# A causal convolution of two runs moved from TensorE to VectorE and GpSimd in a fused attention and gated-linear kernel

## The chip, the cores and the metric

One core of one Trainium2 chip. The metric is device time in microseconds of one execution. Engines are named as the profile names them: PE is TensorE, DVE is VectorE, ACT is ScalarE, POOL is GpSimd, SP is SyncE, which here issues nearly all transfers.

## The reference

Blockwise causal attention over 8 batches, 8 heads, 576 positions and 64 elements per head, then a gated linear unit whose gate comes from a causal depthwise convolution of 5 taps.

```
scores = (q @ k^T) / 8, masked to key block <= query block (blocks of 64)
attn   = softmax(scores) @ v
x      = attn with heads joined: [8, 576, 512]
gate   = sigmoid( sum over k of conv_w[k] * x shifted by 4-k )      # 5 taps per channel
out    = (gate * (x @ w_val)) @ w_out                                # [8, 576, 512], fp32
```

Inputs and output are fp32. The kernel works in fp16 with fp32 accumulation.

## The kernel before, in words

The whole kernel is written out as one list, `PLAN` (lines 12 to 109). Each word of it is one step, name/arguments/engine/banks, and the list is walked once (line 668), so each engine runs its steps in the order in which the list has them. PSUM banks are written into the list too; a step that needs a bank waits until the step that reads the bank's last content is done.

Work on attention goes by pairs of heads, 32 of them: pair p is batch p // 4 and heads 2(p % 4) and the next.

- `lk`, `lq` (line 244), `lv` (260), `lt` (267, the last 64 positions of all heads of a batch, two transfers for q and two for k), `lvt` (274): loads, all issued by SyncE but one (`lq/1`, by ScalarE at the start). The staging tiles rotate: five buffers for q and k, five for v.
- `cq`, `cv`, `ct`, `cvt` (line 232): casts to fp16, mostly on GpSimd.
- `T`, `TT` (141): transposes of q and k on TensorE; `Te`, `TTe` copy them out of PSUM (VectorE or ScalarE).
- `S` (three parts a pair) and `SL`: scores; `E`, `EL` (442, 457): exponentials on ScalarE; `mka`, `mkb` (464 to 470): masking memsets on GpSimd.
- `A`, `AT`: weighted sums with a column of ones that gives the denominator; `N`, `NT` (491, 492): normalization on VectorE; `X`, `XT` and `Xe`, `XTe`: transposes into `xt`.

`xt` holds channels in partitions and positions in a ring of four batches, each with four columns of zeros ahead of it. Work on the gated unit goes by runs of 464 columns of this ring; there are ten runs, n = 0 to 9. Partition 32x + i of group g in `xt` is channel 128g + 32x + i, and the columns of the value and output matrices are ordered to suit the convolution's output (line 383 and the function `W`), where tile x holds the channels of row group x from all four g.

- `C` (line 585): the convolution of a run on TensorE: for each tap 16 matmuls of 32 x 32 blocks with diagonal weights `DG`, 80 in all, into four banks.
- `CS` (598): tanh on ScalarE of two banks at a time into `th` (three buffers, fp32); the sigmoid is made from it.
- `V` (604): value projection, one bank for each of four parts x; `Ve` (612): (th + 1) * value on VectorE into `gv`, which frees the bank.
- `O`, `OL`: output projection from `gv`; `Oe`, `OLe`: copy out of PSUM; `Od`, `OLd`: stores, on SyncE's queue among the loads.
- `w0`: a matmul of zeros that keeps TensorE going; six in the list.

In what follows a step is written as in the list without engine, as in `V/9.3` or `T/30`. Taps of the convolution read `xt` from column 464 (n % 5) on.

Of the kernel before, what the change touches and what calls it, by code (L numbers as in the profile page):

```python
# [17 lines left out]
w0/1.64.1/P/5 E/1.0/A cq/4/V cq/3/V lvt/0/S E/0.2/A lv/2.0/S T/4/P/0+1 lq/8/S lk/8/S lq/7/S
S/1.1/P/2+3 E/1.1/A lk/7/S T/3/P/4+5 S/1.2/P/6+7 E/1.2/A Te/4/V S/4.0/P/0+1 lv/4.1/S T/2/P/2+3
E/4.0/A Te/3/V S/3.1/P/4+5 E/3.1/A mkb/0/G S/3.0/P/6+7 cv/0/G A/0/P/0+1 E/3.0/A S/4.1/P/4+5 Te/2/V  # L20
S/3.2/P/2+3 N/0/V mka/1/G cv/1/V ct/1/G cq/5/G TT/1/P/6+7 TTe/1/V w0/1.64.0/P/0 S/2.2/P/0+1 ct/2/G
E/4.1/A mkb/1/G mka/4/G E/3.2/A X/0/P/4+5 cv/3/G Xe/0/V E/2.2/A cq/6/G mkb/3/G mkb/2/G cvt/0/G
cv/2/G lv/7.0/S lv/5.0/S lv/4.0/S lwv/1/S S/2.1/P/2+3 E/2.1/A lwv/0/S lwo/0/S lwo/1/S T/5/P/4+5
Te/5/V lk/9/S lq/9/S lv/6.0/S lv/5.1/S cq/8/G lv/6.1/S lq/10/S lk/10/S mka/3/G cq/7/G lk/12/S
lq/12/S S/4.2/P/6+7 E/4.2/A mkb/4/G w0/1.64.0/P/0 S/2.0/P/0+1 E/2.0/A SL/1/P/2+3 EL/1/A A/1/P/4+5
N/1/V TT/2/P/6+7 TTe/2/V S/5.0/P/0+1 S/5.2/P/2+3 T/6/P/4+5 Te/6/V lq/13/S X/1/P/6+7 Xe/1/V E/5.0/A
lv/7.1/S lvt/1/S E/5.2/A mkb/5/G AT/0/P/0 NT/0/V lk/11/S lk/13/S lq/11/S S/6.1/P/4+5 S/6.0/P/6+7
SL/2/P/2+3 E/6.0/A EL/2/A T/8/P/0+1 Te/8/V A/3/P/6+7 N/3/V S/5.1/P/2+3 E/6.1/A T/7/P/0+1 Te/7/V
S/8.2/P/4+5 mka/2/G A/2/P/6+7 S/7.1/P/0+1 N/2/V E/5.1/A cwv/1/G cwv/0/G mka/5/G mka/6/G cwo/0/G
X/3/P/2+3 Xe/3/V E/8.2/A X/2/P/6+7 S/6.2/P/4+5 Xe/2/V E/7.1/A S/8.0/P/2+3 E/6.2/A cq/9/G mkb/8/G  # L30
E/8.0/A cv/5/G mkb/6/G cv/4/V C/0/P/0+1+6+7 A/4/P/4+5 XT/0/P/2 V/0.0/P/3 CS/0.1/A N/4/V X/4/P/4+5
CS/0.0/A Xe/4/A Ve/0.0/V S/7.0/P/0+1 E/7.0/A cwo/1/V XTe/0/V V/0.3/P/7 mka/7/G Ve/0.3/V V/0.2/P/3
Ve/0.2/V cv/6/G W//P/0+1+4+5 We/1/V S/7.2/P/6+7 V/0.1/P/2 We/0/A T/9/P/0+1 Te/9/V E/7.2/A
S/8.1/P/4+5 E/8.1/A A/5/P/6+7 S/9.0/P/0+1 A/6/P/4+5 Ve/0.1/V O/0.1/P/2 N/5/V E/9.0/A N/6/V X/5/P/0+1
Xe/5/A cq/10/G T/10/P/6+7 Te/10/V cq/12/G S/9.1/P/4+5 E/9.1/A O/0.2/P/3 Oe/0.2/V T/12/P/0+1 Te/12/V
S/10.0/P/6+7 mkb/7/G cv/7/G E/10.0/A cvt/1/G S/10.1/P/4+5 E/10.1/A O/0.0/P/3 X/6/P/6+7 Xe/6/A
Oe/0.0/A mka/8/G Oe/0.1/A lt/3.0/S lt/3.1/S A/7/P/0+1 AT/1/P/4 lv/8.0/S lt/4.0/S lt/4.1/S
S/12.0/P/6+7 mka/9/G lv/8.1/S N/7/V X/7/P/0+1 NT/1/V cq/11/G Xe/7/V lv/10.1/S E/12.0/A XT/1/P/5
XTe/1/V lv/10.0/S S/9.2/P/2+3 T/11/P/0+1 Te/11/V C/1/P/4+5+6+7 E/9.2/A cq/13/G T/13/P/2+3 V/1.1/P/0
CS/1.0/A lv/9.1/S Te/13/V lv/9.0/S lvt/2/S lv/11.1/S CS/1.1/A S/11.0/P/4+5 S/11.2/P/2+3 ct/3/G  # L40
TT/3/P/6+7 mkb/9/G TTe/3/V Ve/1.1/V cv/8/G V/1.3/P/1 Ve/1.3/V E/11.0/A lv/11.0/S lk/15/S
S/13.2/P/6+7 lq/15/S E/11.2/A S/10.2/P/4+5 mka/10/G lk/16/S V/1.0/P/0 Ve/1.0/V E/13.2/A A/8/P/2+3
N/8/V S/11.1/P/6+7 ct/4/G TT/4/P/0+1 TTe/4/V cv/10/G lq/16/S E/10.2/A lk/14/S lq/14/S V/1.2/P/5
Ve/1.2/V mkb/10/G mkb/11/G A/10/P/2+3 N/10/V mkb/13/G SL/3/P/0+1 E/11.1/A S/13.0/P/6+7 EL/3/A cv/9/G
E/13.0/A cvt/2/G A/9/P/4+5 X/8/P/0+1 Xe/8/A cv/11/G AT/2/P/2 S/12.1/P/6+7 E/12.1/A X/10/P/0+1 N/9/V
mka/11/G A/11/P/4+5 Xe/10/A O/0.3/P/3 NT/2/V XT/2/P/2 XTe/2/A lq/17/S SL/4/P/0+1 EL/4/A cq/15/G
T/15/P/6+7 N/11/V lk/17/S lv/13.1/S Oe/0.3/V S/13.1/P/4+5 Te/15/V O/0.4/P/2 S/12.2/P/0+1 lv/13.0/S
# [6 lines left out]
S/14.1/P/2+3 E/14.1/A Te/18/V V/2.0/P/0 Ve/2.0/V lk/19/S lk/20/S lq/20/S Od/0.2/S lv/16.1/S cv/13/G
mka/13/G A/13/P/4+5 N/13/V S/17.1/P/6+7 Oe/0.5/A mkb/15/G cvt/3/G E/17.1/A S/17.2/P/2+3 V/2.1/P/0
Ve/2.1/V cv/14/G mkb/14/G mka/14/G A/14/P/4+5 S/17.0/P/6+7 cv/12/G E/17.2/A E/17.0/A lv/16.0/S
S/16.2/P/0+1 E/16.2/A N/14/V lq/21/S mkb/12/G A/12/P/2+3 cv/15/G N/12/V lk/21/S ct/5/G AT/3/P/5
S/18.1/P/6+7 E/18.1/A S/16.1/P/2+3 TT/5/P/0+1 TTe/5/V cq/19/G Od/0.1/S lv/18.1/S lt/6.1/S cq/20/G
E/16.1/A mka/16/G cv/16/G O/1.0/P/4 Oe/1.0/V mkb/16/G A/15/P/6+7 T/19/P/0+1 Te/19/A Od/0.4/S
# [24 lines left out]
S/26.1/P/6+7 E/26.1/A NT/5/V V/5.0/P/2 A/23/P/0+1 SL/6/P/6+7 EL/6/A Te/29/V cq/28/G S/26.2/P/3+4
# [28 lines left out]
def kernel(  # L113
# [44 lines left out]
    def one(b):  # L158
        return PS[0:128, b]
# [562 lines left out]
```

## Time and profile before

| | before |
|---|---|
| times of the runs | 186.05, 187.36, 188.68 us (median 187.36) |
| profiled execution: time / span | 188.06 / 186.3 us |
| busy PE / DVE / ACT / POOL | 164.2 / 125.1 / 137.0 / 82.7 us |
| mean granted TensorE clock | 0.972 |
| moved by DMA | 40.38 MB, mean 217 GB/s |
| C: 800 matmuls of 32 x 464 | 13.1 us busy |
| tanh of a half run (`CS`) | 20, mean 945 ns |

The span runs from the first to the last instruction; the time is longer than the span by what the runtime does around it. In the profile's groups, "x40 | 24.6, 633 | 13.1" reads: 40 instructions, 24.6 us busy, 633 ns each, 13.1 us of idle time on the engine just before them, followed by what ended that idle time. A timeline line gives the start and the duration in us, engine, line, operation, tile written <- tiles read. SPq is SyncE's queue: the instruction there issues a transfer, it does not last until the transfer has landed.

### The profile page before, as it was taken

The page shows a single profiled execution, that of the slowest core. Times are in us where ns is not written, and L with a number is a line of the kernel's source. Part 1 is how long each engine was busy: PE and PEld are TensorE (multiplying, and loading weights), DVE is VectorE, ACT ScalarE, POOL GpSimd, SP SyncE. Part 2 cuts the span into 40 slices and gives each one's busy share as a digit, 9 for nine tenths or more (in the row PEclk, how much of TensorE's full clock was granted, in tenths as well). Part 3 has the DMA queues.
Part 4 walks back from the last instruction along what each step waited for, and adds up shares of the span by engine and source line. Part 5 has one row for each costly group of instructions (what it writes and reads, how often), then busy time and mean ns, then how long its engine had stood idle before and what let it go on. Part 6 is the DMA issues. An engine that isn't in the chain of part 4 may idle for free.

```text
span 186.3 us, 8262 instructions
## 1 busy us (share of the span) xinstructions
PE 164.2 (88%) x3534; PEld 101.4 (54%) x3534; DVE 125.1 (67%) x223; ACT 137.0 (74%) x164; POOL 82.7 (44%) x198
## 2 busy tenths in 40 slices
PE   1587638889999996999999999999999999999991
PEld 0364417754565774467645564656665575565540
DVE  5676636749977886777854677799787587533731
ACT  4489963698699885999969998897999842453431
POOL 6206449265682754556407455757590360000000
PEclk9999975699999999999999999999999999999999
DMA  6897896998966899769968888999998110351175
GB/s 184 261 286 180 223 262 172 291 328 243 267 165 157 224 308 300 191 165 327 273 157 272 239 245 260 298 286 282 222 276 231 69 60 0 141 204 57 69 281 217
DMA packets 66493, 40.38 MB, mean 217 GB/s; under 512 B 40213, under 2 KB 60949, under 8 KB 66458
## 3 DMA queue, kind: packets, MB, share of 16 engines
q1 hardware_dynamic: 66186, 39.61, 74.2%
q8 instruction: 27, 0.44, 1.0%
q10 hardware_dynamic: 272, 0.26, 0.4%
q14 instruction: 8, 0.07, 0.1%
HBM read 30.42 MB, written 9.44 MB: 214 GB/s over the span
## 4 chain that ended last, share of the span: by engine, by line
PE 74%; DMA 8%; DVE 5%; ACT 4%; SPq 4%; issue 3%; POOL 1%; DVEq 0%; ACTq 0%; POOLq 0%
PE PS L137 66%; PE PS L141 8%; DMA qks<-in_q_dram 3%; DMA qks<-in_k_dram 3%; ACT pt L442 3%; DMA vs<-in_v_dram 2%; DVE qkT L232 2%; SPq L244 2%; SPq L267 1%; DVE x L492 1%; ACT qkT L230 1%; POOL qk L232 1%; DVE rc L491 0%; DVE kt L232 0%; POOL v L232 0%
## 5 line engine op out<-in xcount | busy, mean ns | idle before, releaser
L442 ACT ACTIVATE pt<-PS 128x1024 f16<-128x1024 f32 x96 | 94.0, 1029 | 16.7 <-PE PS L137 15.1
L232 DVE COPY qkT<-PS 128x1024 f16<-128x1024 f16 x27 | 33.0, 1224 | 14.6 <-PE PS L141 13.7
L232 POOL CAST qk<-qks 128x1024 f16<-128x1024 f32 x28 | 29.1, 1042 | 25.3 <-DMA qks<-in_q_dram 14.8
L137 PE MATMUL PS<-qkT 64*128 64x384 f16 (+3 forms) x256 | 34.4, 319 | 2.9 <-ACT pt L442 1.6
L137 PE MATMUL PS<-xt,w_val 128*128 128x464 f16 x160 | 36.4, 360 | 0.0
L137 PE MATMUL PS<-w_out,gv 128*128 128x512 f16 (+2 forms) x164 | 35.5, 376 | 0.0
L137 PE MATMUL PS<-v,pt 128*128 128x65 f16 (+1 forms) x896 | 32.5, 198 | 2.4 <-POOL v L232 1.4
L137 PEld LDWEIGHTS <-pt 128*128 128x128 f16 (+1 forms) x960 | 29.5, 105 | 8.5 <-issue 4.5
L614 DVE SCALAR_TENSOR_TENSOR gv<-th,PS 128x464 f16<-128x464 f32 x40 | 24.6, 633 | 13.1 <-PE PS L137 7.8
L137 PEld LDWEIGHTS <-qkT 64*128 64x128 f16 x512 | 17.9, 97 | 16.6 <-issue 12.5
L599 ACT ACTIVATE th<-PS 128x928 f32<-128x928 f32 x20 | 17.9, 945 | 7.2 <-PE PS L137 7.0
L492 DVE TENSOR_TENSOR x<-PS,rc 128x512 f16<-128x512 f32 x32 | 22.1, 691 | 1.1
L232 POOL CAST v<-vs 128x512 f16<-128x512 f32 x30 | 18.5, 619 | 7.0 <-DMA vs<-in_v_dram 4.6
L137 PEld LDWEIGHTS <-w_val 128*128 128x128 f16 x160 | 13.5, 97 | 13.0 <-issue 2.4
L137 PEld LDWEIGHTS <-gv 128*128 128x128 f16 (+1 forms) x164 | 12.9, 100 | 12.9 <-issue 1.5
L141 PE MATMUL PS<-ident,qk 64*128 64x64 f16 x512 | 15.6, 202 | 3.3 <-POOL qk L232 3.0
L232 DVE COPY osb<-PS 128x512 f32<-128x512 f32 x20 | 13.7, 687 | 5.8 <-PE PS L137 5.8
L141 PEld LDWEIGHTS <-qk 64*128 64x128 f16 x512 | 12.4, 102 | 8.0 <-POOL qk L232 3.9
L464 POOL MEMSET pt<- 64x256 f16 x32 | 9.8, 306 | 13.3 <-ACT pt L442 12.2
L230 ACT COPY osb<-PS 128x512 f32<-128x512 f32 x15 | 8.7, 591 | 8.6 <-PE PS L137 8.4
L491 DVE RECIPROCAL rc<-PS 128x8 f32<-128x8 f32 x32 | 6.6, 206 | 12.2 <-PE PS L137 6.8
L137 PE MATMUL PS<-xt,DG 32*32 32x464 f16 x800 | 13.1, 358 | 0.4 <-ACT pt L442 0.3
(60 smaller groups left out, 136.4 us busy)
## 6 DMA issues: line engine op xcount, KB each, us to landing
out_dram<-osb SPq DMA_DIRECT2D x35, 256.0 KB, 3.9
qks<-in_k_dram SPq DMA_DIRECT2D x32, 256.0 KB, 4.8
vs<-in_v_dram SPq DMA_DIRECT2D x64, 128.0 KB, 4.4
qks<-in_q_dram SPq DMA_DIRECT2D x31, 256.0 KB, 5.2
tls<-in_q_dram SPq DMA_DIRECT2D x16, 64.0 KB, 3.5
tls<-in_k_dram SPq DMA_DIRECT2D x16, 64.0 KB, 3.6
vts<-in_v_dram SPq DMA_DIRECT2D x8, 128.0 KB, 5.2
gv<-in_moe_w_val_dram SPq DMA_DIRECT2D x2, 512.0 KB, 6.0
```

The lines of the kernel that those rows point to most:

```text
L137: made.append(nc.tensor.matmul(out=out, lhsT=lhsT, rhs=rhs, start=start, stop=stop, skip_group_check=True))
L141: made.append(nc.tensor.transpose(out=out, in_=in_, identity=identity))
L230: i = nc.scalar.copy(out=out, in_=in_)
L232: i = (nc.vector if eng == "V" else nc.gpsimd).tensor_copy(out=out, in_=in_)
L244: DMA[eng].dma_start(out=rot(qks, p)[0:128, i], in_=(q, k)[i][b, 2 * g:2 * g + 2, 0:512, 0:64].rearrange("h (p n) d -> p h (n d)", n=4))
L267: DMA[eng].dma_start(out=tls[b % 2][0:128, i, r], in_=(q, k)[i][b, 0:8, 512:576, 0:64].rearrange("(g r) (p n) d -> r p g (n d)", r=2, n=2)[r])
L442: made.append(nc.scalar.activation(out=rot(pts, p)[0:128, 0:2, 512 * t:512 * t + 512], in_=both(take("S", p, t)), func=AF.Exp, bias=0.0, s ...
L464: nc.gpsimd.memset(pt[64:128, 0:2, 0:1024].rearrange("p h (t s) -> p h t s", t=2)[:, :, :, 0:64], 0.0)
L491: made.append(nc.vector.reciprocal(out=rc[0:128], in_=r[:, :, :, 64:65]))
L492: made.append(nc.vector.tensor_tensor(out=rot(x16, p)[0:128].rearrange("p i h d -> p h i d"), in0=r[:, :, :, 0:64], in1=rc[0:128].to_broad ...
L599: made.append(nc.scalar.activation(out=rot(ths, n)[0:128, 2 * i:2 * i + 2], in_=both(take("C", n, i))[:, :, 0:RUN], func=AF.Tanh, bias=0.0 ...
L614: made.append(nc.vector.scalar_tensor_tensor(out=gv[0:128, x, o:o + RUN], in0=rot(ths, n)[0:128, x], scalar=1.0, in1=one(take("V", n, x))[ ...
```

## The change

Runs 4 and 7 (of 0 to 9) no longer use `C`. For each of the four parts x, four transfers `lx` gather 32 partitions of `xt` from each group g into one tile of 128 partitions, `xp`, so that the convolution of that part becomes five multiply-adds with one scalar per partition and tap. `Q/n.x.kk` is one such tap on VectorE (one instruction; a plain multiply for the first tap) or on GpSimd (a multiply into `part` and an add; the first tap is the multiply alone). The sum stands in `th` in SBUF, and `CS` takes the tanh in place. The scalars `taps` come from a second set of four small matmuls in `CW`. `xp` shares memory with the staging of the convolution's weights, `part` with `olast`.

Of the 40 taps, 19 are on VectorE and 21 on GpSimd. The list is redrawn from its first line: other load order, six warm-up matmuls gone, `lq/1` on SyncE, and steps moved between engines (`Te` on ScalarE 4 to 12 times, `TTe` on ScalarE 0 to 3 times, `Xe` on ScalarE 9 to 2 times).

```
+    pooled = set()
+
+    @op
+    def lx(n, x, eng="S", bank=None):
+        o = RUN * (n % 5)
+        for g in range(4):
+            DMA[eng].dma_start(out=xp[32 * g:32 * g + 32, x],
+                               in_=xt[32 * x:32 * x + 32, g, o:o + RUN + 4])
+
+    @op
+    def Q(n, x, kk, eng, bank=None):
+        pooled.add(n)
+        t = rot(ths, n)[0:128, x]
+        xk, w = xp[0:128, x, kk:kk + RUN], taps[0:128, x, kk:kk + 1]
+        e = nc.vector if eng == "V" else nc.gpsimd
+        if kk == 0:
+            e.tensor_scalar(out=t, in0=xk, scalar1=w, scalar2=None, op0=ALU.mult)
+        elif eng == "V":
+            e.scalar_tensor_tensor(out=t, in0=xk, scalar=w, in1=t, op0=ALU.mult, op1=ALU.add)
+        else:
+            e.tensor_scalar(out=part, in0=xk, scalar1=w, scalar2=None, op0=ALU.mult)
+            e.tensor_tensor(out=t, in0=part, in1=t, op=ALU.add)
+
     @op
     def CS(n, i, eng, bank=None):
+        if n in pooled:
+            t = rot(ths, n)[0:128, 2 * i:2 * i + 2]
+            nc.scalar.activation(out=t, in_=t, func=AF.Tanh, bias=0.0, scale=0.5)
+            return
...
+    stage = const([128, 2048], fp16, "stage")
+    conv_nat = stage[0:5, 0:1024].bitcast(fp32)
+    conv16 = stage[0:5, 1024:1536]
+    conv16x = stage[0:5, 1536:2048]
+    xp = stage[0:128, 0:4 * (RUN + 4)].rearrange("p (x s) -> p x s", x=4)
+    taps = const([128, 4, 5], fp32, "taps")
...
+    part = olast_all[0:128, 0:RUN]
```

The list around run 4, and around run 7 and the end, as it is after the change:

```
+A/14/P/0+1 lk/23/S lt/6.0/S Xe/12/V lv/19.1/S O/0.8/P/6 S/17.2/P/2+3 N/14/V X/14/P/0+1 Xe/14/V
+lx/4.1/S lx/4.0/S lv/19.0/S lk/24/S lq/23/S mka/16/G cv/16/G mkb/16/G A/16/P/4+5 N/16/V lq/24/S
+lx/4.3/S Od/0.4/S cq/21/G E/17.2/A S/20.2/P/0+1 cvt/4/G E/20.2/A lv/18.1/S Od/0.6/S lv/18.0/S
+S/17.1/P/2+3 E/17.1/A V/4.1/P/7 Oe/0.8/V lx/4.2/S C/3/P/0+1+4+5 Od/0.5/S lk/25/S lvt/5/S CS/3.1/A
+T/21/P/2+3 O/0.7/P/6 CS/3.0/A S/18.0/P/4+5 E/18.0/A Te/21/V S/21.1/P/2+3 E/21.1/A Oe/0.7/V
+X/16/P/0+1 mkb/17/G Xe/16/V V/3.0/P/6 mka/19/G cv/17/G cq/22/G Q/4.1.0/V Q/4.0.0/G S/18.2/P/4+5
+E/18.2/A S/20.0/P/0+1 Ve/3.0/V ct/6/G Q/4.1.1/V Q/4.0.1/V lv/21.1/S Q/4.1.2/G V/3.1/P/2 Ve/3.1/V
+V/3.3/P/6 Ve/3.3/V E/20.0/A Q/4.0.2/V SL/5/P/4+5 EL/5/A T/22/P/0+1 Te/22/A Q/4.0.3/V S/21.2/P/2+3
+S/20.1/P/4+5 E/20.1/A V/3.2/P/6 E/21.2/A lv/20.0/S mka/17/G A/17/P/0+1 Q/4.1.3/G S/19.2/P/4+5
+E/19.2/A Ve/3.2/V cq/24/G mka/20/G mka/18/G O/1.1/P/6 Oe/1.1/A Od/1.1/S lq/25/S T/24/P/2+3 N/17/V
...
+cv/31/G A/29/P/4+5 A/28/P/6+7 O/2.6/P/3 mkb/31/G A/31/P/0+1 Oe/2.6/A lx/7.2/S Od/1.2/S lx/7.1/S
+lx/7.3/S Q/7.3.0/G Q/7.3.1/G Q/7.1.0/G N/29/V X/29/P/4+5 N/28/V X/28/P/6+7 Xe/29/V AT/7/P/3
+Q/7.3.2/G Od/2.2/S Xe/28/V O/2.4/P/4 X/30/P/6+7 N/31/V X/31/P/0+1 NT/7/V Q/7.2.0/G Xe/31/V O/1.8/P/5
+XT/7/P/3 Xe/30/V Oe/1.8/A Od/1.8/S V/8.3/P/7 Oe/2.4/A XTe/7/A Q/7.2.1/V Q/7.2.2/V C/8/P/0+1+5+6
+CS/8.1/A Q/7.3.3/V Q/7.3.4/V Q/7.2.3/V Q/7.2.4/V Ve/8.3/V O/2.5/P/3 V/7.1/P/4 CS/8.0/A V/8.0/P/5
+Ve/8.0/V Q/7.0.3/G Q/7.0.4/V C/9/P/0+1+6+7 CS/7.1/A Ve/7.2/V V/8.2/P/5 CS/9.0/A Od/2.4/S CS/9.1/A
+Od/2.3/S V/9.1/P/2 Ve/8.2/V Q/7.1.1/G Q/7.1.2/G Q/7.1.3/G Q/7.1.4/G V/9.0/P/1 Ve/9.0/V V/8.1/P/7
+V/7.0/P/6 CS/7.0/A Ve/7.1/V V/7.3/P/5 Ve/7.3/V Ve/7.0/V Od/2.1/S Od/2.6/S Ve/8.1/V Oe/2.5/A Od/2.5/S
+V/9.2/P/3 Ve/9.2/V V/9.3/P/4 Ve/9.3/V O/3.0/P/1 Oe/3.0/V Od/3.0/S Ve/9.1/V O/3.1/P/5 O/2.7/P/7
```

In this list `lk/30` and `lq/30` are transfers 190 and 186 of SyncE's queue; in the list before they are 169 and 167.

More of the change, by code (lines that the diff above doesn't have):

```diff
@@ L18 @@
[L18 to L29, printed above, removed]
@@ L36 @@
[L36 to L47, printed above, removed]
@@ L54 @@
[L54 to L59, printed above, removed]
@@ L191 @@
     wz = const([128, 512], fp16, "wz")
-    olast = consts(2, [128, 256], fp32, "olast")
+    olast_all = const([128, 512], fp32, "olast")
+    olast = [olast_all[0:128, 256 * i:256 * i + 256] for i in range(2)]
+    part = olast_all[0:128, 0:RUN]
     qks = consts(5, [128, 2, 2, 256], fp32, "qks")
@@ L288, in lcv @@
     def lcv(eng="S", bank=None):
-        DMA[eng].dma_start(out=conv_nat[0:5, 0:512], in_=moe_conv_w[:, :])
+        DMA[eng].dma_start(out=conv_nat, in_=moe_conv_w[:, :])
     @op
@@ L555, in CW @@
                ident16[0:5, 0:5])
+            mm(one(bank)[:, 64 + 16 * g:64 + 16 * g + 5], conv16x[0:5, 128 * g:128 * g + 128],
+               ident16[0:5, 0:5])
     @op
@@ L562, in CWe @@
             in_=r[:, 0:64].rearrange("p (g k) -> p g k", k=16)[:, :, 0:5]))
+        made.append(nc.vector.tensor_copy(
+            out=taps[0:128], in_=r[:, 64:128].rearrange("p (g k) -> p g k", k=16)[:, :, 0:5]))
         nc.vector.tensor_tensor(out=DG[0:128], in0=idfold[0:128].to_broadcast([128, 20, 32]),
@@ L648, in OLe @@
     def OLe(i, eng, bank=None):
-        copy(eng, olast[i][0:128], one(take("OL", i))[:, 0:256])
+        copy(eng, olast[i], one(take("OL", i))[:, 0:256])
     @op
     def OLd(i, eng, bank=None):
-        DMA[eng].dma_start(out=rows(B // 2 - 1, 8)[:, 256 * i:256 * i + 256], in_=olast[i][0:128])
+        DMA[eng].dma_start(out=rows(B // 2 - 1, 8)[:, 256 * i:256 * i + 256], in_=olast[i])
     nc.vector.memset(tiny[0:128], 0.0)
```

152 lines of the change are left out of this document (83 added, 69 removed).

## The prediction, made before the changed kernel was run

> **What bounds the kernel now.** I read the page first, then busy time by stage, then the timelines of SyncE, GpSimd and TensorE around one late pair of heads.
>
> ```profile
> PE 164.2 (88%) x3534; PEld 101.4 (54%) x3534; DVE 125.1 (67%) x223; ACT 137.0 (74%) x164; POOL 82.7 (44%) x198
> ...
> PEclk9999975699999999999999999999999999999999
> DMA  6897896998966899769968888999998110351175
> ```
>
> TensorE is busiest (88%), but no engine is full. The DMA row is as telling: mostly 8 or 9 tenths for three quarters of the span, then a drop. By stage (columns: PE, weight loads, DVE, ACT, POOL, clock, DMA share, GB/s):
>
> ```profile
> 0.00:45.00 45.00, 29.80 (x634) 20.58 (x634) 28.28 (x52) 31.46 (x37) 21.27 (x63) 0.89 0.85 243
> 45.00:100.00 55.00, 52.45 (x1298) 32.91 (x1296) 41.34 (x71) 46.93 (x57) 30.58 (x63) 1.00 0.85 230
> 100.00:142.00 42.00, 41.75 (x913) 24.96 (x912) 32.58 (x57) 38.08 (x44) 25.94 (x58) 1.00 0.96 266
> 142.00:183.00 41.00, 40.20 (x695) 22.91 (x692) 22.93 (x46) 20.49 (x29) 4.90 (x16) 1.00 0.35 125
> ```
>
> From 100 to 142 us TensorE (41.75 of 42), ScalarE (38.08) and the DMA engines (0.96) are all near their limit: a balanced pipeline. After 142 us the loads are over and TensorE alone works off its backlog. How close the loads run to TensorE is seen at pair 30 (its K load from SyncE, its cast, its transposes):
>
> ```profile
> 126.93 0.50 SPq L244 DMA_DIRECT2D qks<-in_k_dram  x1
> ```
>
> ```profile
> 132.58 1.04 POOL L232 CAST qk<-qks 128x1024 f16<-128x1024 f32 x1 [0.34 <-PE PS L137]
> ```
>
> ```profile
> 135.63 0.41 PE L141 MATMUL PS<-ident,qk 64*128 64x64 f16 x16
> ```
>
> ```profile
> qks<-in_k_dram SPq DMA_DIRECT2D x32, 256.0 KB, 4.8
> vs<-in_v_dram SPq DMA_DIRECT2D x64, 128.0 KB, 4.4
> ```
>
> The load lands about 4.8 us after its issue (the median), at 131.7. Cast (1.04) and transposes (135.63) leave 135.63 - 131.7 - 1.04 = 2.9 us to spare. SyncE has no slack either: its timeline shows issues of 0.4 to 0.6 us back to back, up to the last v load at 141.4 us. The order of its instructions shows why: every transfer waits for one of eight semaphores, so at most eight are under way, and 4.4 us / 8 = 0.55 us is the pace whatever their size.
>
> **The change part by part.** The sum is against the profiled execution: span 186.3, time 188.06 us, so 1.76 lies around the span; the median of the runs shown, 187.36, is 0.70 below it.
>
> *Removed on TensorE.* Two of ten convolutions `C`. One costs 1.21 us from its start to the next step's:
>
> ```profile
> 157.57 1.27 PE L137 MATMUL PS<-xt,DG 32*32 32x464 f16 x80
> 158.78 1.54 PE L137 MATMUL PS<-xt,w_val 128*128 128x464 f16 x7
> ```
>
> So 2 x 1.21 = 2.4 us. The six warm-up matmuls `w0` go too (2.1 us busy for the five later ones); those before 25 us lie in start-up idle and count nothing, the two at 70.6 to 72.5 us perhaps 0.8. The start-up order is redrawn as well. I count it at nothing: TensorE already waits there for data (29.8 of 45 us busy), and being early is worth nothing when the loads of late pairs set the pace.
>
> *Added on VectorE.* 19 taps: two runs have 40, GpSimd takes 21. One is a plain multiply, 18 are multiply-adds. Nearest row:
>
> ```profile
> L614 DVE SCALAR_TENSOR_TENSOR gv<-th,PS 128x464 f16<-128x464 f32 x40 | 24.6, 633 | 13.1 <-PE PS L137 7.8 <-ACT th L599 4.3 <-ACT pt L442 0.5
> ```
>
> Same operation and length, one operand in PSUM: 0.63 us; the lower bound is a cast of 512 at 0.42. I take 0.63: 18 x 0.63 + 0.4 = 11.7 us. Moved off VectorE to ScalarE are 8 `Te` (1.22) and 3 `TTe` (0.73); 7 `Xe` (0.42) come back; with the small moves VectorE gains about 3 us, ScalarE 8 x 1.02 + 3 x 0.6 - 7 x 0.59 - 0.4 = 5.5. ScalarE has 4 us idle from 100 to 142 and more before, so I count that at nothing; without this cover it costs up to 5.5.
>
> *Added on GpSimd.* 21 taps: 6 plain multiplies, 15 of a multiply and an add.
>
> ```profile
> L232 POOL CAST qk<-qks 128x1024 f16<-128x1024 f32 x28 | 29.1, 1042 | 25.3 <-DMA qks<-in_q_dram 14.8 <-DMA qks<-in_k_dram 5.8 <-PE PS L137 2.7
> L232 POOL CAST v<-vs 128x512 f16<-128x512 f32 x30 | 18.5, 619 | 7.0 <-DMA vs<-in_v_dram 4.6 <-POOL pt L466 0.9 <-POOL pt L470 0.4
> ```
>
> Between these rows lie 0.83 ns per element, so a multiply of 464 is 0.58 us. The add reads two operands, which no row shows: at least 0.58 (one operand), at most twice a cast of the same 928 elements, 1.9; I take that cast itself, 0.95. A multiply-add is 1.53. Run 4: 2 x 0.58 + 7 x 1.53 = 11.9 us, in a stage where GpSimd is busy 25.9 of 42: 37.8 of 42, just covered. What stands behind a late tap are casts (`cq/24` behind `Q/4.1.3`), and TensorE waits for those. Run 7: after the cast `cv/31`, 3 x 0.58 + 7 x 1.53 = 12.5 us, then `CS` 0.95 and `Ve` 0.63: 14.1. Only then is bank 4, held by `V/7.1`, free for `V/9.3`. TensorE's steps from `A/31` to `V/9.3` (10 `V` of 0.79, 3 `O` of 0.87, 2 `C` of 1.21, the rest 2.4) take 15.3. Hidden, by 1.2 us.
>
> The Trainium skill's page "SBUF — State Buffer" (Who interferes with whom) states that a VectorE instruction with two SBUF inputs and a GpSimd instruction that reads SBUF exclude each other for a whole instruction. By it taps on both engines would take turns with each other and with the casts. In this trace VectorE's two-operand instructions read one operand from PSUM, so no run here shows it; it belongs to the second rival.
>
> *Added on SyncE: the term that decides.* 32 transfers `lx` of 32 rows x 936 B, 30 KB each, 0.96 MB together, 16 of them ahead of the loads of pairs 23 to 31; and `lq/1`, which ScalarE issued. `lx/4.1` also waits for `Xe/14`, with the loads of pairs 19, 23 and 24 behind it, but SyncE runs behind the order there, so I count that wait at nothing (1 to 2 us if it stands). Now count for pair 30. Ahead of its transposes TensorE has the same steps in both orders but for one `C` less, one `A`, one `T`, two `X`, one `XT` more, and the warm-ups: equal within 1 us. But its last load is transfer 169 of SyncE before and 190 after: 16 `lx` and 5 others more. Bounds: by bytes alone, 1.5 MB more at 266 GB/s is 5.8 us; at 0.68 us each (120 issues from 60 to 141.9 us) 14.3. In between, 16 x 0.45 (a bare issue) + 5 x 0.56 = 10.0, which I take, since eight small transfers under way leave the DMA engines little to do. Then the K load lands at 141.7, the cast ends at 142.7, the transposes start 7.1 us later than before.
>
> Behind them lie 186.3 - 135.63 = 50.7 us, now less one `C`, one `A`, one `T`, two `X`, one `XT`: -2.7. Span: 142.7 + 48.0 = 190.7. With 1.76 around it and 0.70 less for the median: **191.8 us**, 4.4 more than now. By bytes alone it is 187.6, at full pace 196.1.
>
> **The rivals.**
>
> 1. *The transfers ride along (other side).* If SyncE's stream has slack that the timeline hides (issues that take 1 to 2.8 us are waits for room, and small transfers land sooner: the two 128 KB `olast` stores at the end needed 2.0 us), the loads of pair 30 come at most 2.9 us later, which their margin takes up. That is the point from which it decides. Then the two `C` come off in full: 186.3 - 2.7 + 1.06 = **184.7**. For it: the 0.45 us issues are shorter than the mean pace. Against: 21 transfers would have to cost under 0.14 us each.
> 2. *GpSimd becomes the bound.* If an add costs 1.9 or the two engines exclude each other, run 4 is 7 x 0.95 = 6.7 longer, 44.5 of 42 us, so casts come some 2.5 us late on top of the loads; and run 7 ends 7 x 0.95 - 1.2 = 5.5 us after TensorE wants bank 4. 191.8 + about 5 = **197**. Against: the tail has idle VectorE time and the add at 0.95 is the nearer row.
> 3. *It does not do what it says.* TensorE's instructions fall by 324 rows (320 for two `C`, 12 for warm-ups, less 8 for the second set of taps), so it does; what may differ is the redrawn start, where the clock was 0.85 (20 to 28 us) and 0.61 (28 to 38). A start without the drop would only let TensorE reach the late loads sooner: about **190**.
>
> **How the numbers follow.** Forecast 0.50; rival 1 0.25; rival 2 0.20; rival 3 0.05. The forecast's own range is 187.6 to 196.1. The range 184.9 to 198.5 takes in the upper part of rival 1 and most of rival 2. Two per cent, 3.7 us, is about what a measurement of this kernel can tell from no change: faster means under 183.6, slower over 191.1. Slower: 0.29 of the forecast, all of rival 2, half of rival 3, 0.52. Faster: 0.08, all from rival 1. Within: 0.40.
>
> **What would show it.** Right: in the profile after, the K load of pair 30 is issued near 137 us instead of 126.93, SyncE's last v load near 150 instead of 141.4, with GpSimd casts waiting for `qks` and TensorE idle for several us between 100 and 145 us, where it had 0.25 in 42. The 80-matmul group appears 8 times. GpSimd adds near 0.95 us and VectorE multiply-adds near 0.63 keep rival 2 away; no TensorE wait ahead of `V/9.3` shows the tail covered. Wrong: the last v load still issued near 142 us (rival 1), or TensorE waiting for VectorE's `Ve/7.1` or for casts that stand behind taps (rival 2).

## The result, and the profile after

The changed kernel takes 219.68 us (219.23 to 221.34, four runs) where the kernel before takes 187.83 beside it: a ratio of 1.168, 95% interval 1.158 to 1.179. The forecast was 191.8, with a range up to 198.5. The sign was right and the size was not: 31.9 us more instead of about 4. All times in what follows are medians of every run; a run more than 1.5% above the fastest of its kernel counts as slow and is left out of the ratios, which leaves one run each of `e2_no_pool_taps` and `e13_casts_first`, too few for a ratio.

The profiled execution of after took 221.34 us, the longest of the four, span 219.6. Its page, the same rows as before (busy time, clock in fortieths of the span, DMA):

```profile
PE 170.8 (78%) x3372; PEld 103.1 (47%) x3372; DVE 134.5 (61%) x241; ACT 142.5 (65%) x167; POOL 133.0 (61%) x233
...
PEclk9999799999999999998599955999999979959999
DMA  5899989988589799855768874961184324200167
```

TensorE has 162 matmuls and 162 weight loads less (3372 of each instead of 3534), the 324 rows that the prediction counted, so the change does what it says. GpSimd is the row that moved: 82.7 to 133.0 us. By stage (columns: PE, weight loads, DVE, ACT, POOL, clock, DMA share, GB/s):

```profile
0.00:45.00 45.00, 31.09 (x678) 20.53 (x680) 27.34 (x54) 36.38 (x42) 25.99 (x69) 0.96 0.90 266
45.00:100.00 55.00, 50.52 (x1190) 31.35 (x1187) 37.48 (x71) 46.21 (x52) 28.41 (x59) 1.00 0.79 208
100.00:142.00 42.00, 27.53 (x460) 15.27 (x461) 24.40 (x39) 21.14 (x25) 34.26 (x41) 0.80 0.76 215
142.00:205.00 63.00, 50.76 (x1000) 30.87 (x1000) 38.68 (x69) 35.59 (x44) 44.31 (x64) 0.92 0.31 91
```

Up to 100 us little has changed. From 100 to 142 us, where TensorE was busy 41.75 of 42, it is busy 27.53, and GpSimd 34.26 instead of 25.94. The last stage, cut at 142 us as before, has become 22 us longer, with GpSimd busy 44.31 instead of 4.90. The granted clock falls to 0.80 and 0.92 in the two stages in which TensorE idles.

The taps, by line (columns: busy, mean ns; then idle before and what ended it), with the multiply-add by which VectorE was costed and the cast rows by which GpSimd was:

```profile
L633 POOL TENSOR_SCALAR olast<-stage,taps 128x464 f32<-128x464 f16 x14 | 21.5, 1538 | 0.7
L634 POOL TENSOR_TENSOR th<-olast,th 128x464 f32<-128x464 f32 x14 | 16.9, 1210 | 1.2
L629 POOL TENSOR_SCALAR th<-stage,taps 128x464 f32<-128x464 f16 x7 | 10.1, 1446 | 8.2 <-DMA stage<-xt 8.1
L631 DVE SCALAR_TENSOR_TENSOR th<-stage,taps,th 128x464 f32<-128x464 f16 x18 | 17.9, 1008 | 20.0 <-POOL th L634 10.6 <-POOL th L629 7.7 <-DMA vs<-in_v_dram 1.6
L657 DVE SCALAR_TENSOR_TENSOR gv<-th,PS 128x464 f16<-128x464 f32 x40 | 24.5, 632 | 14.5 <-PE PS L140 9.3 <-ACT th L640 2.8 <-ACT th L642 1.3
L242 POOL CAST qk<-qks 128x1024 f16<-128x1024 f32 x27 | 28.6, 1063 | 16.8 <-PE PS L140 7.4 <-DVE qk L242 4.4 <-DMA qks<-in_q_dram 2.3
```

A GpSimd multiply of 464 columns takes 1446 ns at the least disturbed line (L629), not the 580 that the casts gave; its multiply-add 1538 + 1210 ns = 2.75 us, not 1.53. The 21 taps (7 plain multiplies and 14 multiply-adds; the forecast had counted 6 and 15, and for run 4 2 and 7 where the list has 3 and 6) are 48.5 us, where the forecast's prices make 7 x 0.58 + 14 x 1.53 = 25.5. VectorE's own multiply-adds take 1008 ns in the mean, not 0.63, and it idles 18 us ahead of them for GpSimd's part of the same sum.

Pair 30 once more (K load issued, cast with its neighbour, transposes):

```profile
140.55 0.44 SPq L254 DMA_DIRECT2D qks<-in_k_dram  x1
```

```profile
153.80 2.03 POOL L242 CAST qk<-qks 128x1024 f16<-128x1024 f32 x2
```

```profile
157.18 0.40 PE L144 MATMUL PS<-ident,qk 64*128 64x64 f16 x16
```

The load was issued at 140.55 (forecast: near 137) and had landed at 144.7, but the cast came 10 us after that. The load is late as forecast, but it is no longer what is waited for: everything ahead of the cast in GpSimd's and TensorE's queues is later still. TensorE's long waits, what VectorE did ahead of the second, and the tail's end, from the timelines of the engines (the bracket is the idle time before and what ended it):

```profile
129.37 1.28 PE L140 MATMUL PS<-v,pt 128*128 128x65 f16 x20 [5.83 <-DVE xt L242]
...
195.25 2.16 PE L140 MATMUL PS<-xt,DG 32*32 32x464 f16 x77 [7.34 <-DVE gv L657]
```

```profile
188.17 6.47 DVE L631 SCALAR_TENSOR_TENSOR th<-stage,taps,th 128x464 f32<-128x464 f16 x6 [5.37 <-POOL th L629]
```

```profile
201.81 1.17 POOL L634 TENSOR_TENSOR th<-olast,th 128x464 f32<-128x464 f32 x1
```

```profile
203.01 0.98 ACT L640 ACTIVATE th<-th 128x928 f32<-128x928 f32 x1 [3.70 <-POOL th L634]
```

Both TensorE waits name VectorE, and both times VectorE had stood at a tap whose sum GpSimd held: 5.70 us before 127.31, ahead of the first, and 5.37 us before 188.17, ahead of the second, where its own six multiply-adds then took another 6.47 us. The last tap ends at 202.98, `CS/7.0` follows at 203.01, then `Ve/7.1` and `V/9.3`.

### The profile page after: what moved, and what is told of

Same layout as the page of the kernel before. It is cut to its first block, busy times and chain, and to the rows that moved or that the text cites. A ratio compares the mean times of both kernels' runs of the same rounds, so it can differ in the third digit from the quotient of the medians.

```text
span 219.6 us, 8066 instructions
## 1 busy us (share of the span) xinstructions
PE 170.8 (78%) x3372; PEld 103.1 (47%) x3372; DVE 134.5 (61%) x241; ACT 142.5 (65%) x167; POOL 133.0 (61%) x233
## 4 chain that ended last, share of the span: by engine, by line
SPq 27%; PE 21%; POOL 19%; DMA 11%; issue 9%; ACT 8%; DVE 3%; POOLq 1%; DVEq 0%; ACTq 0%
PE PS L140 18%; SPq L254 8%; DMA vs<-in_v_dram 7%; SPq L619 6%; ACT pt L454 6%; SPq L270 6%; POOL olast L633 6%; SPq L277 4%; POOL th L634 3%; POOL qk L242 3%; POOL th L629 3%; PE PS L144 2%; POOL v L242 2%; DMA qks<-in_q_dram 2%; DVE qkT L242 2%
## 5 line engine op out<-in xcount | busy, mean ns | idle before, releaser
L140 PE MATMUL PS<-qkT 64*128 64x128 f16 (+3 forms) x256 | 35.6, 328 | 11.1 <-DVE gv L657 4.6
L140 PE MATMUL PS<-xt,w_val 128*128 128x464 f16 x160 | 38.9, 376 | 3.3 <-ACT osb L240 1.7
L140 PE MATMUL PS<-v,pt 128*128 128x65 f16 (+1 forms) x896 | 33.8, 201 | 7.0 <-DVE xt L242 6.0
L242 POOL CAST qk<-qks 128x1024 f16<-128x1024 f32 x27 | 28.6, 1063 | 16.8 <-PE PS L140 7.4
L140 PE MATMUL PS<-w_out,gv 128*128 128x512 f16 (+2 forms) x164 | 36.7, 387 | 2.5 <-DVE gv L657 2.5
L140 PEld LDWEIGHTS <-pt 128*128 128x128 f16 (+1 forms) x960 | 30.8, 106 | 13.2 <-DVE xt L242 5.9
L631 DVE SCALAR_TENSOR_TENSOR th<-stage,taps,th 128x464 f32<-128x464 f16 x18 | 17.9, 1008 | 20.0 <-POOL th L634 10.6
L242 DVE COPY qkT<-PS 128x1024 f16<-128x1024 f16 x19 | 23.1, 1221 | 6.3 <-PE PS L144 6.1
L140 PEld LDWEIGHTS <-w_val 128*128 128x128 f16 x160 | 14.1, 100 | 18.8 <-issue 8.3
L633 POOL TENSOR_SCALAR olast<-stage,taps 128x464 f32<-128x464 f16 x14 | 21.5, 1538 | 0.7
L242 DVE COPY osb<-PS 128x512 f32<-128x512 f32 x19 | 13.0, 687 | 10.5 <-PE PS L140 10.5
L242 DVE COPY xt<-PS 128x512 f16<-128x512 f16 (+1 forms) x34 | 13.4, 405 | 8.0 <-PE PS L144 7.7
L642 ACT ACTIVATE th<-PS 128x928 f32<-128x928 f32 x16 | 14.2, 943 | 5.9 <-PE PS L140 5.8
```

The lines of the kernel that those rows point to most:

```text
L140: made.append(nc.tensor.matmul(out=out, lhsT=lhsT, rhs=rhs, start=start, stop=stop, skip_group_check=True))
L242: i = (nc.vector if eng == "V" else nc.gpsimd).tensor_copy(out=out, in_=in_)
L631: e.scalar_tensor_tensor(out=t, in0=xk, scalar=w, in1=t, op0=ALU.mult, op1=ALU.add)
L633: e.tensor_scalar(out=part, in0=xk, scalar1=w, scalar2=None, op0=ALU.mult)
L642: made.append(nc.scalar.activation(out=rot(ths, n)[0:128, 2 * i:2 * i + 2], in_=both(take("C", n, i))[:, :, 0:RUN], func=AF.Tanh, bias=0.0 ...
```

## Experiments

Theory A: GpSimd's taps are the bound of the two stages, by their price and by what stands behind them. Theory B: the forecast's term, SyncE's transfers delaying the loads. Theory C: VectorE and GpSimd shut each other out of the memory. Theory D: the redrawn order itself is worse. The kernel before, measured beside each group of runs, took 185.75 to 187.17.

**1. Which part of the change costs.**

`e5_order_with_C`: the order alone.

```
- lx/4.* lx/7.* Q/4.* Q/7.*
+ ... Te/22/A C/4/P/0+1+4+5 CS/4.0/A CS/4.1/A ...
+ ... E/31.0/A C/7/P/0+1+4+5 CS/7.0/A CS/7.1/A ...
```

> The changed kernel's order without Q and lx: run 4 and run 7 are convolved by C on TensorE again, each put in by hand where four PSUM banks are free (run 4 behind Te/22, run 7 behind E/31.0). Theory A: the order is not at fault, 186 to 194. Theory D: the redrawn order with its other start-up and no warm-up matmuls carries the loss, 205 or more; a part of it would show as 195 to 204.

Measured 191.54, ratio 1.028 (1.020 to 1.036). The order, with these two `C` put in by hand, costs 5.4 us that the forecast had at nothing; not the 32.

`e2_no_pool_taps`:

```
 def Q(n, x, kk, eng, bank=None):
     pooled.add(n)
+    if eng == "G":
+        return
```

> GpSimd's 21 tap steps are left out of the computation (35 instructions); VectorE's 19, the transfers and the order stay. Theory A: 187 to 194, and VectorE's multiply-adds at 0.70 each with no long ones beside a GpSimd tap. Theories B and D: 213 or more, since transfers and order are the same. If the time is under that of the kernel with all taps on VectorE by several us, VectorE's 13 us more are on the path there.

Measured 191.76 (187.33 to 194.77, a wide spread). Transfers, VectorE's 19 taps, `CS` from the copy and the order are all there: GpSimd's taps alone carry 219.7 - 191.8 = 27.9 us (25 to 32 by the longest and shortest of these runs). Theories B and D fall as the main cause. Theory B is not empty, though. SyncE's timeline in this kernel has the K load of pair 30 at

```profile
136.71 0.43 SPq L254 DMA_DIRECT2D qks<-in_k_dram  x1
```

and in the kernel with the order alone at

```profile
129.70 1.24 SPq L250 DMA_DIRECT2D qks<-in_k_dram  x1
```

7.0 us later with sixteen transfers more ahead of it, and the order alone, with five others more, is 2.8 us behind the 126.93 of the kernel before. The forecast had 7.2 and 2.8, 10.0 in all; measured are 9.8. But that load is not what TensorE waits for. The transposes of pair 30 start at 145.89, 10.3 us later than before (forecast 7.1) and 7.3 later than with the order alone, and GpSimd comes to the cast at 142.52, with its neighbour's, without standing for a load. TensorE's long waits lie at 98 to 114 us, beside the sixteen transfers; there the cast `cq/24` stands for a late Q load and starts at 105.57 instead of 99.74. Two `C` less and a shorter rest behind pair 30 (47.1 us of the profiled span instead of 51.0) take back 3.9 of the 7.3 us. The two profiled executions still lie 3.4 us apart (194.77 and 191.38); the medians, 191.76 and 191.54, do not.

`e1_taps_dve`: all taps on VectorE.

```
- Q/4.0.0/G ... Q/7.1.4/G      # all 21
+ Q/4.0.0/V ... Q/7.1.4/V
```

> All 21 tap steps of GpSimd are given to VectorE; the plan's order and the 32 lx transfers stay. Theory A (GpSimd is the bound in the two stages, because a multiply-add takes it 2.6 to 2.75 us and VectorE's own taps are held up beside it): GpSimd loses the 48.5 us of L629, L633 and L634, VectorE gains 7 x 0.46 + 14 x 0.70 = 13 us and its other 18 multiply-adds fall from a mean of 1008 ns to about 0.70; time 188 to 198. Theory B (SyncE's 32 transfers make the loads late, the term on which the forecast stood): the transfers are all there, so 213 to 220. Theory D (the redrawn order itself is worse): also 213 or more.

Measured 202.3, ratio 1.083 (1.074 to 1.092): between the two expectations. Moving the taps off GpSimd saves 17 us, but VectorE doesn't cover them either: 7 multiplies of 0.47 and 14 multiply-adds of 0.76 us (with no GpSimd tap beside them), 13.9 us in all, cost 10.5 us over the median of the kernel without them.

`e3_no_lx`:

```
 def lx(n, x, eng="S", bank=None):
+    return
...
+ mx//G            # one memset of the copies, in the first half
```

> The 32 lx transfers are left out; the permuted copies are filled once with zeros by GpSimd in the first half, so the taps run on zeros and wait for no transfer. All taps stay where they are. Theory A: the taps' engine time decides, so 210 to 220, little gained. Theory B: the 7 to 10 us of SyncE's stream go and with them the loss, 205 or less.

Measured 210.27, at the edge of what theory A expected: taps on prefilled copies cost most of the loss, but the transfers matter by 9.4 us. Is that SyncE's stream, or the taps that wait for landings?

`e8_lx_unread`: as the last, but the transfers run, into a copy `xq` that nothing reads.

> The 32 transfers run as in the changed kernel, but into a copy that nothing reads; the taps read copies filled once with zeros. With the transfers left out the time was 210.3, with them 219.7. If these 9 us come from SyncE's stream (theory B, as a smaller part), the time stays near 219. If they come from GpSimd and VectorE standing at the transfers' landing with casts queued behind (theory A: an engine that takes its work in order), it is near 210.

Measured 212.46, ratio 1.141 (1.133 to 1.149). 7.2 of the 9.4 us are the waiting for the landing; the other 2.2, the stream, lie within the spread of `e3_no_lx` (207.49 to 210.98). GpSimd stood 8.1 us at L629 in after (the group above), with casts behind it.

`e4_before_lx`: the kernel before plus the 32 transfers, into a copy that nothing reads.

```
- ... Xe/16/V lv/19.0/S lk/23/S Od/0.6/S ...
+ ... Xe/16/V lx/4.1/S lx/4.0/S lv/19.0/S lk/23/S lx/4.3/S Od/0.6/S ...
- ... lv/30.0/S Oe/2.4/V ...
+ ... lv/30.0/S lx/7.0/S lx/7.2/S lx/7.1/S lx/7.3/S Oe/2.4/V ...
```

> The kernel before with nothing but the 32 transfers added at the like places of SyncE's queue, into a copy that nothing reads. Theory B (the forecast's deciding term: 10 us of later loads, 7 us at the transposes of pair 30): 190 to 196. Theory A (transfers alone are carried along): 185 to 189.

Measured 208.43, ratio 1.120 (1.110 to 1.129): both theories missed it. It has two parts. The first is the forecast's term by itself, the K load of pair 30 (126.93 before) and its transposes (135.63 before):

```profile
133.05 0.50 SPq L244 DMA_DIRECT2D qks<-in_k_dram  x1
```

```profile
142.39 0.41 PE L141 MATMUL PS<-ident,qk 64*128 64x64 f16 x16
```

Sixteen transfers make the load 6.1 us and the transposes 6.8 us later. The other 12.2 us of the 19.0 by which the profiled span is longer come behind pair 30, from run 7's transfers, which stand ahead of the stores. SyncE, VectorE and TensorE in the late stage:

```profile
150.38 21.49 SPq L603 DMA_DIRECT2D xp<-xt  x16
171.91 0.58 SPq L649 DMA_DIRECT2D out_dram<-osb  x1
```

```profile
174.28 0.69 DVE L232 COPY osb<-PS 128x512 f32<-128x512 f32 x1 [10.87 <-DMA out_dram<-osb]
```

```profile
175.02 3.25 PE L137 MATMUL PS<-xt,w_val 128*128 128x464 f16 x8 [9.41 <-DVE osb L232]
```

The 16 transfers of run 7 wait in SyncE's queue for the last `Xe` that they read (`Xe/26`, done at 162.18) and then take 9.7 us to issue; the stores stand behind them for 21 us in all, so no output buffer comes free, so VectorE can't empty a bank, so TensorE waits 9.4 us. In the order of the change the same 32 transfers stand elsewhere, and `e2_no_pool_taps` takes 191.76 with them.

**2. Price or lost cover.** GpSimd's 35 tap instructions on fewer columns, all else as in after (the edit in short form):

```
+ if eng == "G":      # multiplies on m columns, adds on a
+     m, a = 186, 376                       # e9_forecast_prices
+     m, a = 112, 361                       # e15_exact_prices
+     m, a = 16, 16                         # e12_tiny_pool_taps
```

> GpSimd's taps work on fewer columns, so that each costs about what the forecast took for it: multiplies on 186 of 464 columns (1447 x 186/464 = 580 ns if the price goes with the columns), adds on 376 (1168 x 376/464 = 946 ns); the other columns are left out of the convolution. VectorE's taps, transfers and order as in the changed kernel. Theory A with the forecast's structure right: near the forecast's 191.8, within 189 to 196. If it stays over 200, the price alone is not what failed, and GpSimd is the bound even at the prices that the forecast took.

> All of GpSimd's 35 tap instructions are there, with their waits for the transfers' landing and for VectorE, but on 16 of 464 columns; the rest is left out of the convolution. If the price of the instructions makes the loss, the time is that without them, 189 to 194. If waiting in GpSimd's queue is a cost of its own (the 7 us between transfers read and unread), 196 to 202. With it the slope between 32 us of taps (208.0) and none (191.8) is parted into price and wait.

> The changed kernel with GpSimd's multiplies on 112 columns (0.305 us + 112 x 2.46 ns = 0.58, the forecast's price) and its adds on 361 (0.95); the other columns are left out. From the runs with 13.1, 32.0 and 48.5 us of GpSimd taps (194.6, 208.0, 219.7) a straight line gives 203 at 25.5 us: then 16 us of the miss are the price and 11.6 are work that the forecast called hidden and that is not. If the forecast's cover holds at its own prices: 190 to 195.

| | GpSimd tap time | time |
|---|---|---|
| none (`e2_no_pool_taps`) | 0 | 191.76 (187.33 to 194.77) |
| `e12_tiny_pool_taps` | 13.1 us | 194.58 |
| `e15_exact_prices` | 27.9 us | 202.84 |
| `e9_forecast_prices` | 32.0 us | 207.96 |
| after | 48.5 us | 219.68 |

The column of tap times is the sum of the three groups in each trace. `e12_tiny_pool_taps` lies between its two expectations. In `e9_forecast_prices` the price did not shrink with the columns (921 ns for a multiply instead of 580: there is a fixed part, and VectorE beside it), so it was not at the forecast's prices; `e15_exact_prices` nearly was (565, 749 and 965 ns in the mean; 27.9 us of taps where the forecast's prices make 25.5). The first 13 us of tap time cost 2.8 us, which is within the spread of the kernel without taps; from there on each us of GpSimd time costs 0.7 us in the mean, (219.68 - 194.58) / (48.5 - 13.1), though not evenly: 0.56, 1.25 and 0.71 from point to point. So of the 27.9 us between no taps and after some 16.8 are the price (219.7 - 202.8), and 11.1 (8 to 15.5 by the spread) are work at about the forecast's own prices, which it called hidden.

**3. Where: the two stages.**

`e6_run4_taps_only` and `e7_run7_taps_only`: one run by taps, the other by `C` in its place as above.

> Run 4 by taps as in the changed kernel, run 7 by C on TensorE, put in by hand behind E/31.0. From the changed kernel's windows about half of the loss lies in run 4's stage (TensorE idle 14 of 28 us) and half in run 7's: 203 to 208. If taps cost only in the late stage, where nothing is left to hide them, 192 to 196; if run 4 carries nearly all, 215 or more.

> Run 7 by taps as in the changed kernel, run 4 by C on TensorE, put in by hand behind Te/22. Run 4's taps cost 204.95 - 191.54 = 13.4 us by the runs so far. If the two stages add up, run 7's cost the other 14.7: 206. If a late run 4 also pushes run 7's taps into the end (the stages feed each other), run 7 alone costs less: 196 to 202.

Measured 204.95 (1.097, 1.088 to 1.107) and 204.32 (1.100, 1.089 to 1.110). Over the order alone: run 4 13.4, run 7 12.8; together 26.2 of the 28.1 that separate after from it. The two stages nearly add up.

`e14_run4_tiny`: the first of these with GpSimd's nine steps on 16 columns.

> The kernel with run 4 alone by taps, GpSimd's nine steps of it on 16 of 464 columns (the rest left out). Transfers, waits and VectorE's taps stay. Without GpSimd's price: 191 to 195, so that 10 to 13 of run 4's 13.4 us belong to it. If it stays over 199, the transfers and the queue's waits make run 4's loss.

Measured 193.39, ratio 1.038 (1.030 to 1.047): 11.6 of run 4's 13.4 us are GpSimd's time, 1.8 are left for transfers, waits and VectorE's taps.

`e13_casts_first`: again run 4 alone, with the taps behind the casts.

```
- cq/22/G Q/4.1.0/V Q/4.0.0/G ... Q/4.1.3/G ... cq/24/G ... cq/23/G ...
+ cq/22/G ... cq/24/G ... cq/23/G Q/4.1.0/V Q/4.0.0/G ... Q/4.1.4/V ...
- ... Q/4.2.0/G Q/4.3.0/G ... Q/4.2.4/V CS/4.1/A ... cq/25/G ... cq/26/G ...
+ ... cq/25/G ... cq/26/G lv/22.1/S lq/27/S Q/4.2.0/G Q/4.3.0/G ... Q/4.2.4/V CS/4.1/A cv/22/G ...
```

> From the kernel with run 4 alone by taps (204.95; run 7 by C). Run 4's taps of columns 0 and 1 are moved as a block behind the cast cq/23 (GpSimd had three of them ahead of cq/24), those of columns 2 and 3 behind cq/26; CS/4.1 moves with them, TensorE's order is the same. If casts standing behind taps in GpSimd's queue make run 4's loss, the loads' chain is freed and the time falls to 193 to 199. If GpSimd's total time in the stage makes it, or the late Ve of run 4 takes the place of the late casts, it stays at 202 to 210.

Measured 218.89 (215.59 to 220.04): outside both expectations, 14 us worse than with taps ahead of casts. TensorE's timeline has the new wait:

```profile
144.39 1.92 PE L138 MATMUL PS<-w_out,gv 128*64 128x512 f16 x8 [15.13 <-DVE gv L655]
```

From 127.17 to 141.6 us GpSimd does nothing but taps, and TensorE waits 15.1 us for run 4's `Ve`. So the casts behind the taps are not *the* cause: GpSimd's queue has a deadline on both sides of the taps, the casts of the next pairs behind them and the gate of run 4 after them, and the 21 us of run 4's taps (9.4 + 7.2 + 4.3 in `e6_run4_taps_only`) fit in neither of the two places tried. A finer mixture of taps and casts was not tried; of what was, only less GpSimd time helped.

**4. The prices by themselves, and the lock.**

`e10_no_dve_taps`: VectorE's 19 steps return at once.

> VectorE's 19 tap steps are left out of the computation, GpSimd's 21 stay, with transfers and order. Theory A (GpSimd's own time and its queue): GpSimd's multiplies fall from a mean of 1538 ns to the undisturbed 1447 and its adds from 1210 to 1168, 2 us in all, and the time stays at 210 to 218. Theory C (the two engines shutting each other out of the memory is the main cost): the lock is gone, 200 or less.

Measured 218.0, ratio 1.171 (1.161 to 1.182). With VectorE out of the way GpSimd's multiplies take 1442 ns and its adds 1165, as expected, and it saves 1.7 us. Theory C is a side effect. The run shows more: no sum passes between the two engines any longer, and VectorE stands at no tap, yet the time is nearly the same. TensorE's waits have only changed their names. Two of them:

```profile
123.74 1.26 PE L140 MATMUL PS<-v,pt 128*128 128x65 f16 x20 [6.45 <-POOL v L242]
...
199.10 3.25 PE L140 MATMUL PS<-xt,w_val 128*128 128x464 f16 x8 [9.32 <-ACT osb L240]
```

The first waits for a cast of v behind the taps, the second for a copy that stands on ScalarE behind `CS/7.0`, which waits for GpSimd's last tap. So the wait of VectorE for GpSimd, by which the loss is seen in after, is not what makes it; GpSimd's own queue is.

`e11_prices`: behind the last copy of the kernel before, three of each on 464 columns (in short form):

```
+ G.tensor_scalar(out=f32, in0=f16, scalar1=sc, ...)     # L702; 0.25 for sc: L704
+ G.tensor_copy(out=f32, in_=f16)                        # L706
+ G.tensor_scalar(f16 <- f16), (f32 <- f32)              # L708, L710
+ G.tensor_tensor(f32 <- f32,f32), (f32 <- f16,f32)      # L712, L714
+ G.tensor_scalar(...) on 186 columns                    # L718
+ V.scalar_tensor_tensor(...) x4 alone, x6 beside G      # L721, L726 beside L724
```

> The kernel before with a series of single instructions on 464 columns behind its last copy, GpSimd alone first; the time is not to be compared. For GpSimd: the multiply with a per-partition scalar, fp16 to fp32, should give the 1447 ns of the taps. If the per-partition scalar makes it dear, the multiply by a constant and the plain copy come to 0.4 to 0.9 us; if it is the width of the types, the fp16-to-fp16 one is cheaper than the fp32 one; if every GpSimd pass over 464 columns costs 1.2 us or more, all are alike and no cast row could have stood for it. 186 columns: 920 ns as in the run with shortened taps. VectorE's multiply-add: 0.69 us alone; beside GpSimd multiplies it should end with each of them, 1.4 us, if the two exclude each other, and stay at 0.69 if not.

From its groups (mean ns of one behind the comma):

```profile
L702 POOL TENSOR_SCALAR th<-w_val,wsc 128x464 f32<-128x464 f16 x3 | 4.3, 1446 | 0.3
L704 POOL TENSOR_SCALAR th<-w_val 128x464 f32<-128x464 f16 x3 | 4.1, 1369 | 0.3
L706 POOL CAST th<-w_val 128x464 f32<-128x464 f16 x3 | 1.7, 574 | 0.2
L708 POOL TENSOR_SCALAR w_out<-w_val,wsc 128x464 f16<-128x464 f16 x3 | 4.3, 1444 | 0.2
L710 POOL TENSOR_SCALAR th<-th,wsc 128x464 f32<-128x464 f32 x3 | 4.3, 1445 | 0.2
L712 POOL TENSOR_TENSOR th<-th 128x464 f32<-128x464 f32 x3 | 3.5, 1160 | 0.2
...
L721 DVE SCALAR_TENSOR_TENSOR th<-w_val,wsc,th 128x464 f32<-128x464 f16 x4 | 2.8, 702 | 0.1
...
L724 POOL TENSOR_SCALAR th<-w_val,wsc 128x464 f32<-128x464 f16 x4 | 6.7, 1674 | 0.4
L726 DVE SCALAR_TENSOR_TENSOR th<-w_val,wsc,th 128x464 f32<-128x464 f16 x6 | 5.0, 836 | 0.8 <-POOL th L722 0.7
```

None of the three guesses at the cause holds: not the per-partition scalar (1369 with a constant), not the types (1444, 1445, 1446), and not every pass (the cast takes 574, just the 0.58 that the forecast had read off the casts). It is this instruction, `tensor_scalar` with a multiply, whatever it reads: 2.5 times a cast of the same tile. Whether a multiply by another instruction, or another operation in this one, is cheaper was not tried. On 186 columns it took 762 ns, so about 0.3 us are fixed and 2.46 ns go with each column. VectorE's multiply-add takes 702 ns alone and 836 beside GpSimd, GpSimd's multiply 1674: they hold each other up, but far from whole instructions. Four multiplies and six multiply-adds, one after the other, would be 4 x 1.45 + 6 x 0.70 = 10.0 us; side by side they took 7.0.

## Why the prediction failed, step by step

- *Multiply on GpSimd, 0.58 us: the step that failed most.* The cast rows priced a cast rightly (574 ns) and were taken for another operation. Measured 1446. The add was 0.95 us, measured 1.16 alone; its bounds (0.58 to 1.9) held. No upper bound was kept for the multiply at all, and so the range had no place for it. By the runs in part 2 the prices make some 16.8 us.
- *Run 4, "37.8 of 42, just covered".* At about the forecast's own prices the two runs together still cost 11.1 us (`e15_exact_prices`), so the cover failed apart from the price; how the 11.1 divide between run 4, run 7 and the waits for the landing was not measured. The 42 us were an average; GpSimd's taps don't start before 101.7 (the landing of `lx/4.0`), their results are wanted by run 4's gate, and the casts of pairs 23 and 24 fall in between. At the true price it is 25.9 + 3 x 1.45 + 6 x 2.6 = 45.9 of 42 by the same sum, 4 us over, and run 4 cost 13.4: the average is too kind by most of it. In `e13_casts_first` the one other place tried in the queue cost 14 us more.
- *Run 7, 14.1 against 15.3, "Hidden, by 1.2 us".* At the measured price the same sum comes near. GpSimd's ten taps lasted from 177.6 (the last memset behind `cv/31`) to 202.98, 25.4 us instead of 12.5; 12.9 more, less the margin of 1.2, is 11.7; the runs gave 12.8. What waited was not only `V/9.3`: `C/9` stood 7.34 us at 187.9, because `Ve/8.3`, which frees its bank, stands behind VectorE's taps, and those behind GpSimd's. The prediction named what is behind a GpSimd tap, not what is behind a VectorE tap that waits for one. Without VectorE's taps (`e10_no_dve_taps`) a copy behind `CS/7.0` makes TensorE wait instead, so it is the end of GpSimd's taps that counts, not the queue that passes the wait on.
- *VectorE's multiply-add, 0.63.* 0.70 alone, 1.01 in this kernel beside GpSimd. The idle time ahead of them, 18 us, is as large as their 17.9 us of work. The 11.7 us that the forecast added on VectorE never entered its sum, and no cover for them was worked out. For these 19 taps that did no harm that the runs show (191.76 with them and the transfers, 191.54 with `C` in place of both), but `e1_taps_dve` pays 10.5 us for 21 more.
- *SyncE's stream, the deciding term: right in size, wrong in place, and not what decided.* With GpSimd's taps out the load of pair 30 was issued at 136.71 ("near 137"), 9.8 us later than before (forecast 10.0), and the kernel before with the transfers alone has it 6.1 us later. An `lx` took 0.59 us to issue, not the 0.45 of the sum. But TensorE didn't wait for that load; it had lost its time at 98 to 114 us. That the kernel without GpSimd's taps takes 191.76, the forecast's 191.8, is luck in good part: its runs go from 187 to 195, and the sum has the order, 5.4 us, at nothing. Waits for the landing, at `L629`, were not in the sum; they cost 7.2 in the kernel with all taps.
- *Order and start, counted at nothing:* 5.4 us, with two `C` placed by hand, so not all of it need be the order's. Rival 3's start without the clock's drop did come (0.96 in the mean of the first 45 us instead of 0.89), and made nothing faster.
- *Rival 2* named the right mechanism, its place and the sign to look for, TensorE waiting behind taps, and priced it at 5 us with a chance of 0.20, since only the add was thought uncertain. Neither of its conditions came true, an add of 1.9 us or engines that exclude each other: its sign came true by a price that it hadn't doubted. By the Trainium skill's page "SBUF — State Buffer" (Who interferes with whom), as the prediction cites it, the ten instructions side by side in `e11_prices` would have taken turns, 10.0 us; they took 7.0, so here the measurement decides, and taking VectorE's taps away gave 1.7 us. The Trainium skill's page "GPSIMD Engine Reference" (Engine selection) holds one-input operations on GpSimd to be roughly at line rate and two-input ones about twice as slow as VectorE's. Here GpSimd's one-input multiply takes 1446 ns where VectorE's took 462 in after, and GpSimd's two-input add takes 1160 (no run here has VectorE's): by that page the same step would have failed.
- *Rival 1* (transfers ride along, 184.7) is refuted by the load of pair 30, 6.1 us late with the transfers alone and its transposes 6.8; even a perfect cover would have gained only 2 x 1.21 us, 1.3%, less than a measurement of this kernel tells from no change.

## What to carry to other kernels

Price an operation by a row of the same operation on the same engine, and where there is none, keep an upper bound for every one of them, not for the one that looks odd. Busy time against a stage's average is no cover for work in a queue that runs in order: ask when its first input lands, who wants its last result, and what stands behind it meanwhile; here GpSimd time cost 0.7 us per us although GpSimd was only 44% busy in the kernel before. The engine that a wait names need not be its cause: with VectorE's taps away TensorE waited for others, and the time stayed. And weigh the ceiling first: 2.4 us of TensorE were bought with 48 us of GpSimd, 18 of VectorE and 32 transfers.

## What was not expected of the hardware

- On GpSimd a multiply by a scalar (1446 ns for 464 columns) is dearer than an add of two tensors (1160) and 2.5 times a cast (574), with each of the three pairs of types tried.
- VectorE and GpSimd beside each other: VectorE's multiply-add from 702 to 836 ns, GpSimd's multiply from 1446 to 1674. In after single VectorE multiply-adds reached 1600 ns beside GpSimd's adds; whether adds hold VectorE up longer than multiplies was not measured by itself.
- A transfer from one tile to another of 32 rows x 936 B takes 0.59 us to issue and 1.9 to land, so 16 of them keep a queue that issues in order for some 10 us, and anything behind them too.
- A wait of TensorE cost more than its length. From 183.5 to 187.5 us of after its granted clock was 1.00, and 80 matmuls of `C/8` took 1.27 us; after the wait of 7.34 us the clock was 0.50 (195.2 to 197.5 us), and 77 matmuls of `C/9` took 2.16. In `e13_casts_first`, behind the wait of 15.13 us, it was 0.50 too (146.2 to 148.4 us), and 80 took 2.16.
